# The first pair's down product as seven block products in a second last stage

## The chip, the cores and the metric

One core of a Trainium2 chip runs the whole kernel. The metric is the device time of one execution in microseconds. Five engines run side by side, each in the order of its own queue, and wait for one another by semaphores: TensorE (PE in the profile, with PEld for its weight loads), VectorE (DVE), ScalarE (ACT), GpSimd (POOL) and SyncE (SP), which here only issues transfers. A transfer between DRAM and SBUF is issued by SP, or by ScalarE's queue, and moved by 16 DMA engines.

## The reference

A transformer block on 2048 tokens of width 512 with six modulation vectors made from `c`: layer norm, linear attention with 32 heads, a gated residual, layer norm again, and a bilinear feed-forward part with 1376 hidden columns, again with a gated residual. The change touches the last part alone:

```python
h = _layernorm(x, axis=-1) * (1 + cb) + sb
g = jnp.einsum("bsd,df->bsf", h, w_gate)
u = jnp.einsum("bsd,df->bsf", h, w_up)
x = x + gb * jnp.einsum("bsf,fd->bsd", g * u, w_down)
```

All is float32.

## The kernel before

**Split operands.** A float32 operand is split into a high part (a copy into the fp32r type, on ScalarE) and a low part (the difference, on VectorE or GpSimd). A product is three matmuls: high by high, high by low, low by high (`split`, L201).

**Chunks, pairs, f tiles.** The tokens are four chunks of 512 (four tiles of 128). The hidden columns are eleven f tiles, 0 to 9 of 128 and 10 of 96. For the first pair of chunks (0, 1) the f tiles 8, 9 and 10 are done earlier, chunk by chunk (`gate_up`, `down`). The rest runs in the generator `ffn` (L1316): eight steps for the first pair with f tiles 0 to 7, then eleven steps for the second pair (2, 3) in the order `LATE`.

**A step** (`block`, L1183) makes gate and up of one f tile for both chunks of a pair. Two by two blocks (chunk by half of the width on the left, half of the width by gate or up on the right) are multiplied with seven block products where the plain way has eight. Each is six matmuls (`times`, L1160): a step has 42. Its left operands, "side parts", are a11, a12, a22 and the sums s1 to s4, each for two k tiles and in two parts. Its right operands, a "right", are b11, b21, b22 and the differences t1 to t4, held in seven tiles. A step uses four PSUM banks a, b, c, d: ScalarE copies a to b, b to c, and d and b to SBUF, VectorE adds and multiplies. With `raw` the result h stays whole, otherwise it is split by `flush` at the next step. The set of banks is `banks`, or `others` where `on` says so.

**Points and plan.** After each of the seven products the generator yields; the points "p1", "p5", "p6", "p2", "p7", "p3", "p4" are the places after product 1 to 7 at which `more` and `plan` put other work. `gates` (L1302) puts there: at p7 the load of the right of step m + 2 and the split of that of step m + 1, at p4 the differences of that of step m + 2 (GpSimd). In the first pair's steps p1 parks the right in DRAM (seven transfers); `Fetched` reads it back for the second pair.

**The first pair's down product.** After every two steps `down_group` (L1240) multiplies the two f tiles of h by w_down, plainly, 24 matmuls of 512 columns per chunk, and `evac` adds the result to x on VectorE; the groups of chunk 0 and chunk 1 are put behind later steps. The rows of w_down are loaded by `draw_load`, scaled by `gb` on VectorE, split on ScalarE and GpSimd.

**The second pair** keeps the h of all eleven f tiles. `planned` (L1497) puts the preparation of its w_down parts at points of its steps: five pairs of f tiles, each made into b11, b21, b22, t1 to t4 and parked. Its side parts a11, a12, s1, s2, s3 are also parked in DRAM (`aside`, `stash`) during the first pair's steps and read back before its own. `run` (L1576) is the last stage: its seven block products over five pairs of f tiles, six in a turned form with 512 columns (`turned`, L1481), the last with 256 columns (`product`, `mm`, L1461). For the turned ones the result is turned back by 32 by 32 blocks and moved by blocks to the output, after x was read back the same way (`x_blocks`, `flip`, `finish`). Its fetches from DRAM all go through SP's queue, in the order of the code.

Of the kernel before, what the change touches and what calls it, by code (L numbers as in the profile page):

```python
# [8 lines left out]
F32 = mybir.dt.float32  # L9
# [15 lines left out]
def tile_adaln_block(  # L25
# [1214 lines left out]
    def down_group(ch, side, js, outs, ds, last, by_tile=False, end=False):  # L1240

        hs = [out[side] for out in outs]

        def mm(ps, i, j, c, d):
            (hh, hl), (dh, dl) = hs[i], ds[i]
            a, b = j * P, (j + 1) * P
            n = hh.shape[0]
            nc.tensor.matmul(ps, hh[:, a:b], dh[:n, c:d], start=i == 0, stop=False)  # L1248
            nc.tensor.matmul(ps, hh[:, a:b], dl[:n, c:d], start=False, stop=False)  # L1249
            nc.tensor.matmul(ps, hl[:, a:b], dh[:n, c:d], start=False, stop=i == len(hs) - 1)  # L1250

        dn = {j: acc_bank() for j in js}
        tail = js[-1:] if end else []
        order = [(i, j) for i in range(len(hs)) for j in js if j not in tail]
        if by_tile:
            order.sort(key=lambda ij: ij[1])
        for i, j in order:
            mm(dn[j], i, j, 0, D)

        def take():  # L1260
            evac(ch, dn, [j for j in js if j not in tail], last)
            for j in tail:
                other = acc_bank()
                for ps, c, d in ((dn[j], 0, D // 2), (other, D // 2, D)):
                    for i in range(len(hs)):
                        mm(ps[:, c:d], i, j, c, d)
                    evac(ch, {j: ps}, [j], last, ((c, d),))
        return take

    groups = [((0, 1), g) for g in ((0, 1), (2, 3), (4, 5), (6, 7))]  # L1270
    steps = [(cs, f) for cs, g in groups for f in g]
    LATE = (10, 8, 9, *range(8))
    FIRST_AGAIN = len(steps) + 3
    steps += [((2, 3), f) for f in LATE]
    rights = {}

    def right_load(n):
        if n < FIRST_AGAIN:
            rights[n] = Right(steps[n][1])

    def right_sums(n, on=None):
        if n < FIRST_AGAIN:
            rights[n].sums(on)

    def right_split(n, on=None):
        if n < FIRST_AGAIN:
            rights[n].high()
            rights[n].lows(on)

    draws = {}  # L1290

    def draw_load(n):
        if n < len(steps):
# [626 lines left out]
```

## Time and profile before

| | us |
|---|---|
| median of three runs | 537.68 (537.64 to 537.89) |
| profiled execution | 538.41 |
| its span in the trace | 536.3 |
| TensorE busy | 530.6 |
| first pair's steps, with what runs among them | 251.7 to 363.3 |
| last stage, its first to its last matmul | 479.1 to 532.7 |

The profile's times count from the start of the span. The granted clock of TensorE was 1.00. A group of instructions is told by its line, engine, operation and operands, with its count, busy time and mean duration; a row of a timeline has start, length, engine, line and count; "SPq" is SP issuing a transfer, and "idle before" names what ended the wait.

### The profile page before, as it was taken

To read this page: it belongs to the slowest core of one execution; us is meant where nothing else is said; L and a number is where in the kernel's file an instruction comes from. 1 tells how busy PE (TensorE), PEld (TensorE's weight loads), DVE (VectorE), ACT (ScalarE), POOL (GpSimd) and SP (SyncE) were. 2 spreads that over 40 slices of the span, in tenths; PEclk is the share of its full clock that TensorE was granted. 3 is DMA by queue.
4 is the path that set the end of the run, shared out by engine and by line. 5 is a ranking of instruction groups with operands and counts; after the bars stand their busy time and mean duration, and the time that the engine had idled before them with its cause. 6 is when DMAs were issued, how large, how long until landed. Compare 5 with 4: busy or idle time off the path is not lost.

```text
span 536.3 us, 7850 instructions
## 1 busy us (share of the span) xinstructions
PE 530.6 (99%) x2407; PEld 436.9 (81%) x2407; DVE 406.3 (76%) x692; ACT 308.4 (58%) x584; POOL 157.0 (29%) x169
## 2 busy tenths in 40 slices
PE   8999999999999999999999999999999999999997
PEld 6888888888878878878888888887888888888886
DVE  7998878999999888779766577895646465569584
ACT  3696878769577774577584544554433434345530
POOL 2001010000012220076696677655632222310000
PEclk9999999999999999999999999999999999999999
DMA  8912426220075255857869687797189999589875
GB/s 271 385 50 76 160 94 212 89 78 2 30 210 177 61 199 154 281 167 217 275 187 337 227 297 238 261 350 232 61 281 326 400 383 367 198 265 285 268 166 140
DMA packets 102489, 113.39 MB, mean 211 GB/s; under 512 B 26480, under 2 KB 57712, under 8 KB 102448
## 3 DMA queue, kind: packets, MB, share of 16 engines
q1 hardware_dynamic: 98096, 111.85, 63.4%
q10 hardware_dynamic: 4352, 1.05, 0.9%
q8 instruction: 19, 0.31, 0.2%
q14 instruction: 22, 0.18, 0.1%
HBM read 68.03 MB, written 44.83 MB: 210 GB/s over the span
## 4 chain that ended last, share of the span: by engine, by line
PE 93%; DVE 4%; ACT 2%; issue 0%; ACTq 0%; DVEq 0%
PE bank L1165 27%; PE acc L882 8%; PE acc L1165 7%; PE bank L1489 4%; PE acc L1489 4%; PE bank L217 3%; PE bank L216 3%; PE bank L215 3%; PE acc L1249 3%; PE acc L1248 3%; PE acc L1250 3%; PE acc L424 3%; PE acc L423 3%; PE acc L422 3%; PE bank L965 2%; PE bank L967 2%
## 5 line engine op out<-in xcount | busy, mean ns | idle before, releaser
L1165 PE MATMUL bank<-h,w 128*128 128x512 f32 (+1 forms) x630 | 145.3, 389 | 0.0
L1165 PEld LDWEIGHTS bank<-h,w 128*128 128x128 f32 (+1 forms) x630 | 117.0, 186 | 25.9
L1170 ACT ACTIVATE bank<-bank 128x512 f32<-128x512 f32 (+1 forms) x32 | 18.7, 584 | 76.7 <-PE bank L1165 73.4
L203 DVE TENSOR_TENSOR kl<-u,kh 128x512 fp32r<-128x512 f32 (+1 forms) x38 | 26.4, 742 | 29.7 <-ACT kh L202 24.5
L271 POOL TENSOR_TENSOR rstd<-ve,half 128x2 f32<-128x2 f32 (+3 forms) x13 | 11.8, 910 | 108.1 <-DVE ve L270 64.9
L217 PE MATMUL bank<-w,h 128*128 128x512 f32 x104 | 40.7, 391 | 0.0
L215 PE MATMUL bank<-w,h 128*128 128x512 f32 x104 | 40.7, 391 | 0.0
L216 PE MATMUL bank<-w,h 128*128 128x512 f32 x104 | 40.5, 390 | 0.0
L1165 PE MATMUL acc<-h,w 128*128 128x512 f32 x168 | 38.7, 389 | 0.0
L203 POOL TENSOR_TENSOR w<-raw,w 128x512 fp32r<-128x512 f32 (+1 forms) x15 | 22.3, 1494 | 51.6 <-ACT w L202 46.5
L882 PE MATMUL acc<-w,xh 128*128 128x512 f32 x120 | 37.3, 392 | 0.0
L1165 PEld LDWEIGHTS acc<-h,w 128*128 128x128 f32 x168 | 31.5, 188 | 6.5
L1127 POOL TENSOR_TENSOR w<-raw,w 128x256 fp32r<-128x256 f32 (+3 forms) x22 | 24.3, 1104 | 37.2 <-ACT w L1120 37.2
L952 DVE TENSOR_TENSOR x<-acc,x 128x512 f32<-128x512 f32 x40 | 26.4, 685 | 11.1 <-PE acc L1250 11.1
L1127 POOL TENSOR_TENSOR w<-t,w 128x512 fp32r<-128x512 f32 (+1 forms) x22 | 29.2, 1329 | 0.0
L882 PEld LDWEIGHTS acc<-w,xh 128*128 128x128 f32 x120 | 22.4, 188 | 5.0 <-DVE w L793 0.3
L422 PE MATMUL acc<-kh,xh 128*128 128x512 f32 x64 | 25.1, 393 | 0.0
L424 PE MATMUL acc<-kl,xh 128*128 128x512 f32 x64 | 25.0, 390 | 0.0
L423 PE MATMUL acc<-kh,xl 128*128 128x512 f32 x64 | 25.0, 390 | 0.0
L1248 PE MATMUL acc<-w,kh 128*128 128x512 f32 x64 | 24.9, 389 | 0.0
L1250 PE MATMUL acc<-w,kl 128*128 128x512 f32 x64 | 24.9, 389 | 0.0
L1249 PE MATMUL acc<-w,kh 128*128 128x512 f32 x64 | 24.9, 389 | 0.0
(265 smaller groups left out, 1304.6 us busy)
## 6 DMA issues: line engine op xcount, KB each, us to landing
right<-w SPq DMA_DIRECT2D x56, 256.0 KB, 3.8
w<-right SPq DMA_DIRECT2D x56, 256.0 KB, 5.1
raw<-in_w_mod_dram SPq DMA_DIRECT2D x24, 256.0 KB, 4.0
raw<-in_B_w_down_dram SPq DMA_DIRECT2D x20, 256.0 KB, 4.0
down_t<-w SPq DMA_DIRECT2D x20, 256.0 KB, 5.1
w<-down_t SPq DMA_DIRECT2D x20, 256.0 KB, 5.3
x<-in_A_x_dram SPq DMA_DIRECT2D x16, 256.0 KB, 5.5
down_b<-w SPq DMA_DIRECT2D x15, 256.0 KB, 5.2
```

The lines of the kernel that those rows point to most:

```text
L203: (low or nc.vector).tensor_tensor(l, src, f32(h), op=ALU.subtract)
L215: nc.tensor.matmul(ps, ah, bh, start=i == 0, stop=False)
L216: nc.tensor.matmul(ps, ah, bl, start=False, stop=False)
L217: nc.tensor.matmul(ps, al, bh, start=False, stop=i == n - 1)
L422: nc.tensor.matmul(tacc[k], xh[:, a:b], kh, start=first, stop=False)
L423: nc.tensor.matmul(tacc[k], xl[:, a:b], kh, start=False, stop=False)
L424: nc.tensor.matmul(tacc[k], xh[:, a:b], kl, start=False, stop=last)
L882: nc.tensor.matmul(yps[i], x, y, start=False, stop=k == KD - 1 and x is al, skip_group_check=True)
L1127: sub = lambda out, x, y: (on or nc.gpsimd).tensor_tensor(out, x, f32(y), op=ALU.subtract)
L1165: mm = lambda x, y, **kw: nc.tensor.matmul(ps, x[:, k], y, skip_group_check=True, **kw)
L1248: nc.tensor.matmul(ps, hh[:, a:b], dh[:n, c:d], start=i == 0, stop=False)
L1489: nc.tensor.matmul(ps, of[:, x], y, start=start, stop=False, skip_group_check=True)
```

## The change

The eight f tiles of the first pair are no longer multiplied by w_down in groups between the steps. Each step's h (two tiles) is parked in DRAM. After the second pair's last stage a second one, `run_late`, multiplies them by the second pair's parked w_down parts: four pairs of f tiles ((0, 1), (2, 3), (4, 5), (7, 6)), seven block products. Four are "narrow": three matmuls of 256 columns for each pair and token tile. Three are "wide": one of 512 columns (the high part of h against both parts of w side by side) and one of 256, the two halves being added by VectorE. The results are added to x by half rows and stored.

With it come:

- the order `LATE` starts with f tile 7, whose right stays in SBUF (`KEPT`); the pair (7, 6) comes last
- the first pair's h is `raw`; its odd steps from the fourth on use `others`
- the second pair's side parts go into SBUF (`split_in`) and are not parked
- x of chunk 0 is parked in DRAM early and read back in the last stage
- the low parts of the rights of steps 4 and 6, of the odd f tile's w_down and of its first pair's parts are made on VectorE, not on GpSimd; the low parts of every other pair in the late stage on GpSimd
- all w_down parts are stored in the order that the turned form needs; the additions of the narrow products undo it by a stride of two
- in `run`, the late stage's first operands are fetched (a11 and b11 after the fourth product is issued; a12, a21, b21, a22 and x of chunk 0 after the sixth), a11 is split, and s1 and s3 are made by VectorE among its last additions

```diff
-    groups = [((0, 1), g) for g in ((0, 1), (2, 3), (4, 5), (6, 7))]
-    steps = [(cs, f) for cs, g in groups for f in g]
-    LATE = (10, 8, 9, *range(8))
-    FIRST_AGAIN = len(steps) + 3
-    steps += [((2, 3), f) for f in LATE]
+    FIRST = tuple(range(8))
+    LATE = (7, 10, 8, 9, *range(7))
+    ODD, LAST = 10, (7, 6)
+    steps = [((0, 1), f) for f in FIRST] + [((2, 3), f) for f in LATE]
+    FIRST_AGAIN = len(steps) - 7
+    KEPT = len(FIRST)
...
-            rights[n].lows(on)
+            rights[n].lows(nc.vector if n in ON_VECTOR else on)
+    ON_VECTOR = (4, 6)
...
-        if free[0] and parts:
-            takes = [down_group(*p) for p in parts.pop(0)]
-            yield
-            for take in takes:
-                take()
+    def h_park(f, out):
+        h_parked[f] = []
+        for n, x in enumerate(out):
+            h_parked[f].append(tc.dram_tile([P, D], F32, name=f"h_{f}_{n}"))
+            nc.sync.dma_start(h_parked[f][n], x)
...
+        pairs = list(zip(LATE[2:-1:2], LATE[3:-1:2])) + [LAST]
+        wide_down = Down((2, 3), pairs, KEPT)
+        late_down = Down((0, 1), pairs[1:], KEPT, wide_down)
...
+        for m, (cs, f) in enumerate(steps[:KEPT]):
+            out = []
+            more = {}
+            if m < KEPT - 1:
+                more["p1"] = [lambda: rights[m].park(f)]
+            if m:
+                more["p5"] = [lambda: h_park(*before)]
+            if m == 2:
+                others.extend(acc_bank() for _ in range(4))
+            yield from gates(m, cs, side, out, more, raw=True, on=others if m > 2 and m % 2 else None)
+            before = f, out
...
-        wide_down.run()
+        wide_down.run(late_down)
+        late_down.run_late(others[2:])
...
+        def h_fetch(self, n, side):
+            for fs in self.fs:
+                self.h.setdefault(fs[n], [None] * 2)[side] = load(h_parked[fs[n]][side], "u")
...
-                split(self.a(i, name), h, l)
+                split(self.a(i, name), h, l, nc.gpsimd if self.of and i % 2 else None)
...
             self.turned(d, "s1", "t1", True)
+            then.h_fetch(0, 0)
+            then.w_fetch("b11")
             self.h_split("s3", *pairs)
...
             self.turned(d, "s4", "b22", False, (0, 1))
+            then.h_fetch(1, 0)
+            then.h_fetch(0, 1)
+            then.w_fetch("b21")
+            then.h_fetch(1, 1)
+            xts[then.cs[0]] = [load(to, "x") for to in x_parked]
             self.finish(p5, c1, 1, nc.scalar)
             u2 = self.flip(onto(d, u2))
             self.finish(u2, c0, 1, nc.scalar)
+            then.h_split("a11", *range(then.NI))
...
                         if i % 2 == 0:
                             nc.sync.dma_start(ov(c1, i)[:, :HALF], x(i))
+                    for i in range(then.NI):
+                        then.h_sum("s1", i)
+                        then.h_sum("s3", i)
             add(*before)
+
+        def run_late(self, C):
...
+            self.h_split("a12", *pairs)
+            self.w_fetch("t2")
+            narrow("a11", "b11", True)
+            self.drop("a11", "b11")
+            self.h_next("s2", 0, 1)
+            add(c0, 0, C, js)
+            self.w_fetch("t1")
+            wide("a12", "b21", True)
+            self.drop("a12", "b21")
+            self.h_next("s2", 2, 3)
+            add(c0, 0, A, js, True)
+            self.w_fetch("t3")
+            narrow("s2", "t2", False)
+            self.drop("s2", "t2")
+            self.h_split("s1", *pairs)
+            add(c0, 1, C, js)
+            self.w_fetch("b22")
+            wide("s1", "t1", True)
+            self.drop("s1", "t1")
+            self.h_split("s3", *pairs)
+            self.h_next("s4", 0)
+            add(c1, 1, A, js)
+            self.w_fetch("t4")
+            narrow("s3", "t3", False)
+            self.drop("s3", "t3")
+            self.h_next("s4", 1, 2, 3)
+            add(c1, 1, C, js, True)
+            wide("s4", "b22", False)
+            self.drop("s4", "b22")
+            self.h_split("a22", *pairs)
+            add(c0, 1, A, js, True)
+            before = []
+            for j in (0, 2, 1, 3):
+                narrow("a22", "t4", False, (j,))
+                add(c1, 0, C, before, True)
+                before = (j,)
+            add(c1, 0, C, before, True)
```

More of the change, by code (lines that the diff above doesn't have):

```diff
@@ L1238, in block @@
         yield
[L1240 to L1268, printed above, removed]
@@ L1299, in tile_adaln_block @@
     free = [False]
-    parts = []
     def gates(m, cs, A, out, more, raw=False, on=None):
@@ L1342, in ffn @@
         for n, f in enumerate(LATE):
+            m = KEPT + n
             out = wide_down.h.setdefault(f, [])
[L1344 to L1348 removed]
+            more = {}
+            if n == 0:
+                more["p5"] = [lambda: h_park(*before)]
```

135 lines of the change are left out of this document (72 added, 63 removed).

## The prediction

> **What bounds the kernel now.** I read the page first, then the chain of work that ended last in order of time, then the instructions of one engine after another in the last 60 us, and the busy time by stretches.
>
> ```profile
> span 536.3 us, 7850 instructions
> PE 530.6 (99%) x2407; PEld 436.9 (81%) x2407; DVE 406.3 (76%) x692; ACT 308.4 (58%) x584; POOL 157.0 (29%) x169
> ...
> L1248 PE MATMUL acc<-w,kh 128*128 128x512 f32 x64 | 24.9, 389 | 0.0
> L1250 PE MATMUL acc<-w,kl 128*128 128x512 f32 x64 | 24.9, 389 | 0.0
> L1249 PE MATMUL acc<-w,kh 128*128 128x512 f32 x64 | 24.9, 389 | 0.0
> ```
>
> TensorE is busy for 99% of the span. The 389 ns of one matmul overlap with the next, so the price of a matmul is read from the chain, where runs of them stand with start, length and count:
>
> ```profile
> 259.87 23.12 PE bank L1165 x102
> ...
> 288.43 9.52 PE bank L1165 x42
> ...
> 303.38 9.53 PE bank L1165 x42
> ...
> 469.55 9.52 PE bank L1165 x42
> 479.06 3.40 PE acc L1489 x15
> ...
> 524.06 8.63 PE acc L1468 x72
> 532.72 0.42 DVE x L1639
> ```
>
> A step of the gate and up products (42 matmuls of 512 columns) takes 9.52 us, 0.2267 us each. From 288.43 to 303.38 there are 14.95 us: 42 matmuls of a step and 24 of the down groups (66 x 0.2267 = 14.96). So TensorE never waits between these steps; a wait that the change brings is paid in full. The 72 matmuls of 256 columns at L1468 take 8.63 us, 0.1199 us each, a little over half of 0.2267.
>
> **The change: TensorE.** Removed are the 64 + 64 + 64 = 192 matmuls of the first pair's down product: 192 x 0.2267 = 43.53 us. Added are seven products of four f pairs and four token tiles. Four are narrow: 4 x 4 x 4 x 3 = 192 matmuls of 256 columns. Three are wide: 3 x 16 = 48 of 512 columns (high part of h against both parts of w) and 48 of 256. That is 240 x 0.1199 + 48 x 0.2267 = 28.78 + 10.88 = 39.66 us. TensorE saves 3.87 us. Widths of 512 and 256 in turn don't stand in this trace. From below such a pair costs one and a half of 0.2267, 0.3400; from above two of it, 0.4534. I take the sum of the two rows, 0.3466, nearest to which both kinds stand by themselves; the ends are 0.3 us less and 5.1 us more over 48 pairs.
>
> By the Trainium skill, "TensorE: Matmul & The Clock Gate", section "Back-to-back issue gap", a matmul of N columns follows the one before after N/2.4 + 2.5 ns, that is 215.8 and 109.2 ns; the saving would then be an estimated 41.4 - 36.6 = 4.9 us. The trace disagrees with both gaps (226.7 and 119.9 ns), and the trace is used.
>
> The end stays: after the last matmul one 256-column add and its store, as now (532.72 to the span's end at 536.3).
>
> **First stage: less cover for the same side work.** Without the down groups the eight first steps last 9.52 us each where they had about 15. The stretch below holds the y products and steps 0 to 7 with their down groups.
>
> ```profile
> core 0: us, PE busy (x) PEld busy (x) DVE busy (x) ACT busy (x) POOL busy (x), PEclk, DMA share, GB/s
> 251.70:363.30 111.60, 111.60 (x494) 92.24 (x493) 83.54 (x124) 61.89 (x117) 73.55 (x69) 1.00 0.82 276
> ...
> 402.90:460.00 57.10, 57.10 (x254) 47.28 (x253) 31.64 (x53) 22.47 (x49) 15.90 (x22) 1.00 1.00 366
> ```
> ```profile
> L952 DVE TENSOR_TENSOR x<-acc,x 128x512 f32<-128x512 f32 x25 | 16.5, 686 | 5.7 <-PE acc L1250 5.7
> L203 DVE TENSOR_TENSOR kl<-u,kh 128x512 fp32r<-128x512 f32 x14 | 11.1, 834 | 9.5 <-ACT kh L202 9.5
> ...
> L203 DVE TENSOR_TENSOR h<-s,h 128x512 fp32r<-128x512 f32 x11 | 9.4, 880 | 0.1
> ...
> L1328 DVE TENSOR_TENSOR raw<-raw,row 128x512 f32<-128x512 f32 x8 | 5.3, 667 | 0.0
> ```
> ```profile
> L203 POOL TENSOR_TENSOR w<-raw,w 128x512 fp32r<-128x512 f32 x8 | 12.6, 1581 | 0.0
> ```
>
> It shrinks to about 2.7 + 8 x 9.52 = 79 us. VectorE loses the additions to x (L952, 16.5), the low parts of h (11.1) and the scaling of w_down (5.3), and takes over the low parts of two rights (8 operations, some 5 us): 83.5 - 32.9 + 5 = 56 of 79 us. ScalarE loses the copies that go before these low parts. GpSimd loses the 8 w_down splits (12.6) and two rights' low parts (some 9): 52. None becomes the bound on average. The transfers lose 28 side tiles (14 out, 14 back) and 8 of w_down, and gain 14 parked h tiles; at 0.262 MB a tile 276 GB/s x 111.6 us = 30.8 MB become about 25. By the row a full share moves 276/0.82 = 337 GB/s, so 25 MB take 74 of 79 us: nearly full, as the second stretch already is (share 1.00) without a wait of TensorE. The queue of SP is the thing to follow: it issues in order, and a right's loads stand behind the parking of another right.
>
> ```profile
> 286.01 4.25 SPq L1142 DMA_DIRECT2D right<-w  x7
> 290.35 0.84 SPq L116 DMA_DIRECT2D raw<-in_B_w_down_dram  x1
> 291.28 0.40 SPq L1103 DMA_DIRECT2D raw<-in_B_w_gate_dram  x1
> ```
> ```profile
> raw<-in_B_w_gate_dram SPq DMA_DIRECT2D x20, 128.0 KB, 3.8
> ...
> u<-stowed SPq DMA_DIRECT2D x8, 256.0 KB, 5.0
> ```
> ```profile
> 295.72 1.30 POOL L1127 TENSOR_TENSOR w<-t,w 128x512 fp32r<-128x512 f32 x1
> ...
> 300.73 0.74 POOL L1109 TENSOR_TENSOR t<-raw 128x256 f32<-128x256 f32 x1
> ```
>
> Take right 5. Two h tiles replace the w_down load ahead of it, so its four loads end at 293.7 and land 3.8 us later, at 297.5. GpSimd (right 4's low parts are now VectorE's) does four differences at about 0.72 by 300.4, then the low parts at 0.72 and 1.25 each: b11 at 301.1, t1 and t2 at 302.4. Step 5 begins at 251.71 + 2.72 + 5 x 9.52 = 302.0 and needs b11's low part two matmuls later, at 302.5: 1.3 us to spare. A landing after 5.0 us instead of 3.8 just eats that; I take 0.3 us for the whole stage, with 0 and 2.7 us as ends. The side parts of the second pair keep their place by step, so they are now made in less time: step 6 has four operations on banks at 0.69 and eight sums and low parts at 0.88 (the h<-s row), 2.8 + 7.0 = 9.8 us of VectorE in 9.52; step 7 has 2.8 + 7 x 0.88 = 9.0 and makes the 0.3 good. Alternate steps use other banks, so TensorE does not feel that lag: 0, and up to 1 us.
>
> **The handover, where I expect the price.** The late stage's second product reads the parts of a12, whose low parts VectorE makes after eight sums (s1, s3) that need the a21 and a22 halves of h, fetched from DRAM. These fetches are put on SP's queue behind the last moves of the stage before.
>
> ```profile
> GB/s 271 385 50 76 160 94 212 89 78 2 30 210 177 61 199 154 281 167 217 275 187 337 227 297 238 261 350 232 61 281 326 400 383 367 198 265 285 268 166 140
> ```
> ```profile
> 480.95 6.24 SPq L1413 DMA_DIRECT2D w<-down_t  x10
> ...
> 504.22 2.28 SPq L1413 DMA_DIRECT2D w<-down_t  x5
> 506.55 9.35 SPq L1550 DMA_DIRECT2D x<-x_rows  x16
> 517.00 3.85 SPq L1550 DMA_DIRECT2D c<-t  x8
> 520.96 4.26 SPq L116 DMA_DIRECT2D u<-c  x4
> ```
> ```profile
> w<-down_t SPq DMA_DIRECT2D x20, 256.0 KB, 5.3
> ...
> c<-t SPq DMA_DIRECT2D x8, 64.0 KB, 1.8
> ```
> ```profile
> 481.24 3.09 DVE L203 TENSOR_TENSOR kl<-u,kh 128x512 fp32r<-128x512 f32 x5
> ...
> 527.21 0.41 DVE L1639 TENSOR_TENSOR x<-x,acc 128x256 f32<-128x256 f32 x1
> 528.40 0.42 DVE L1639 TENSOR_TENSOR x<-x,acc 128x256 f32<-128x256 f32 x1 [0.78 <-PE acc L1468]
> 528.74 1.42 DVE L1650 TENSOR_TENSOR x<-x,u 128x256 f32<-128x256 f32 x4
> ```
>
> All in the old trace's clock. Eight new issues (a11 and b11 of the late stage) stand ahead of the 504.22 row; at its 2.28/5 = 0.456 us each that is 3.65 us. So x_rows ends at 515.90 + 3.65 = 519.5, c<-t (ready since 517.0) at 523.4, u<-c at 527.6. Then come 16 fetches of 256 KB: a12, a21, b21, a22. At 400 GB/s, which the slices of the page reach in the long stretch of fetches, one takes 0.655 us; with 1.8 us for the first, the landing time of c<-t, the sixteenth lands at 527.6 + 1.8 + 15 x 0.655 = 539.2. VectorE meanwhile reaches the sums at about 530.4 (the 528.74 row's end after two low parts at 3.09/5 = 0.62 more, of which the 0.78 idle takes a part) and would be through at 535.3. With the last tile at 539.2 the last two sums end at 540.5, two additions of 0.33 behind them at 541.1 and a12's first low part at 541.8. TensorE ends its first late product at 532.69 + 48 x 0.1199 = 538.45 and wants that part one wide matmul later, at 538.7. Wait: 541.8 - 538.7 = 3.1 us. What is queued behind the sums on VectorE are the last two additions of the second pair and all low parts that TensorE asks for; TensorE waits for these.
>
> The ends of this cost: if SP does not slip (u<-c at 525.2) and issues at 0.456, the sixteenth lands at 525.2 + 16 x 0.456 + 1.8 = 534.3, before VectorE is through, and the wait is 0 (below nothing it can't go, the product isn't shortened). If 16 issues go at 6.24/10 = 0.62 and the last lands 5.3 later, it is there at 527.6 + 9.3 + 5.3 = 542.2, and the wait is 6.0. I take 3.1, which goes by the rate of the transfers themselves.
>
> Behind it: VectorE has 8 sums of 0.62, 16 low parts of 0.62 (8 go to GpSimd) and 40 half additions of 0.33 in 39.7 us, 28 us; each next operand is then 1.4 to 2.5 us early. I take 0 there, up to 1.
>
> Sum, against the profiled execution of 538.41 (536.3 and 2.1 around it): 538.41 - 3.87 + 3.1 + 0.3 = 537.94. That execution lies 0.73 above the median 537.68, so on the median's scale **537.2**.
>
> **Rivals.** Fetches in time: the wait at the handover is 0 to 1.2 us and the first stage waits nowhere. For it: 402.90 to 460.00 shows full transfers and no wait; against it: 28 new issues on a queue that is already busy there. 537.68 - 3.87 + 0.3 = 534.1.
>
> Slower, by the supply of rights in the first stage: a step now carries 7 + 2 tiles and 0.52 MB of loads, 2.88 MB or 8.5 us at 337 GB/s; step 3 has the 1.05 MB that are fetched back for the flips (11.6 us) and step 5 the stores of x (10.1 us). If loads queue behind these stores for the excess over 9.52, 2.1 + 0.6 = 2.7 us come on top of the 3.1: 537.68 - 3.87 + 3.1 + 2.7 = 539.6. It decides once a right lands 1.3 us later than counted. Against it: parking may lag without harm, and no right is loaded for step 8.
>
> Slower, by a colder TensorE after the handover: the trace has such a start once.
>
> ```profile
> 2.00 8.44 PE acc L149 x24
> ```
>
> The first 24 matmuls of the kernel, of 512 columns, took 0.352 us each, 3.0 us more than 24 x 0.2267. If a wait of 4.2 us (the landing 1.1 later than taken) is followed by such a start: 537.68 - 3.87 + 4.2 + 3.0 + 0.3 = 541.3. Nothing in the trace shows whether a pause of that length does it. The same page of the Trainium skill, section "Part 1: The HAM clock gate", says that a pause of about 3.4 us or more halves the clock; by that rule the 3.1 taken stays just short of it.
>
> That the change doesn't save what it says: not likely, since both widths are in the trace.
>
> **How the numbers follow.** Forecast (handover wait between 1.8 and 4.5): 0.40, its own range 535.9 to 538.6. In time: 0.30. Supply of rights: 0.20. Cold start: 0.10. A measurement of this kernel tells from no change about 0.2%, 1.1 us: faster is under 536.6, slower over 538.8. Faster: 0.30 and a quarter of the forecast's 0.40 make 0.40; slower: 0.30 and a little of the forecast's late end, 0.32; within: 0.28. Range 533.9 to 541.0.
>
> **What would show it.** Right: steps 0 to 7 at 9.52 us without a gap; matmuls of the late products at 0.120 and 0.227; one gap of TensorE of about 3 us at the second late product, ended by a low part of VectorE that stood behind sums waiting for a fetched tile. Wrong: no gap there (then 534), gaps at the starts of steps 3 to 7 ended by GpSimd or a right's load (then 539 or more), or first matmuls after the gap at twice 0.2267.

## The result, and the profile after

The changed kernel takes 567.0 us (median of four runs, 565.54 to 567.69) beside 537.67 us of the kernel before on the same chip: ratio 1.0541, 95% interval 1.052 to 1.0562. The forecast was 537.2, its range 533.9 to 541.0. The profiled execution is the one of 567.69 us, with a span of 566.0.

From its page, the head, the busy time of TensorE and two rows of the forty slices:

```profile
span 566.0 us, 8107 instructions
...
PE 532.2 (94%) x2503; PEld 440.6 (78%) x2503; DVE 421.5 (74%) x727; ACT 312.5 (55%) x588; POOL 143.4 (25%) x154
...
PE   8999999999999999999998999989999999905997
...
PEclk9999999999999999999998999999999999966999
```

TensorE is busy for 532.2 us but for 94% of the span: it waits some 34 us, most of it in one place, slices 36 and 37, where the granted clock falls as well. The chain of waits has the place (start, length, what):

```profile
445.31 3.40 PE acc L1463 x15
...
490.31 4.31 PE acc L1442 x36
...
504.34 5.31 DMA u<-h
509.67 3.12 DMA out_dram<-t
512.80 1.66 ACT kh L202 x3
...
515.74 0.42 DVE x L1628
516.21 11.19 PE acc L1442 x80
...
545.55 5.75 PE acc L1442 x48
551.30 0.23 PE bank L1671
...
556.95 5.77 PE acc L1442 x48
```

The span is split at the first matmul of the last two stages. Before, that is 479.06, or 435.53 once the removed 43.53 us of down groups are taken out; from there 57.24 us are left, or 96.90 with the 39.66 us of the added products. After, it is 445.31 with 120.7 us left. So the first part lost 9.8 us and the last two stages 23.8: -3.87 + 9.8 + 23.8 = 29.7, the difference of the spans. The 3.87 goes into this split as it was forecast; that it is there is seen from the products themselves. A narrow one takes 5.75 us (the row at 545.55), and a wide one 5.65 us (from 551.30 to 556.95, sixteen pairs of a 512 and a 256 at 0.353): 4 x 5.75 + 3 x 5.65 = 39.95 us where 39.66 were forecast. In all runs below these two numbers are given: the start of the last two stages (435.5 would be no loss) and what follows it (96.9).

**The handover.** Four engines around the gap, from the timelines of the changed kernel:

```profile
494.33 0.28 PE L1442 MATMUL acc<-w,kl 96*128 96x256 f32 x1
516.21 0.79 PE L1442 MATMUL acc<-w,kh 128*128 128x256 f32 x2 [21.60 <-DVE x L1628]
...
513.44 0.69 DVE L203 TENSOR_TENSOR kl<-u,kh 128x512 fp32r<-128x512 f32 x1 [19.90 <-ACT kh L202]
...
515.74 0.74 DVE L1628 TENSOR_TENSOR x<-x,acc 128x256 f32<-128x256 f32 x2
...
487.61 25.12 ACTq L1530 DMA_DIRECT2D out_dram<-t  x16
512.78 3.75 ACT L202 ACTIVATE kh<-u 128x512 fp32r<-128x512 f32 x7 [29.98 <-DMA out_dram<-t]
...
494.98 4.02 SPq L116 DMA_DIRECT2D u<-h  x8
...
504.94 2.40 SPq L116 DMA_DIRECT2D x<-x  x4
```

Read backwards: TensorE waits for an addition of the second pair (L1628), which frees a bank. It stands on VectorE behind two low parts of the late block's a11; they wait for ScalarE's high parts; and ScalarE, which had nothing to compute, stands for 25.12 us in sixteen output transfers (L1530). p5's eight run from 487.6 to 493.5; u2's eight are issued only from 507.7 on, after the last of SP's fetches (507.34). The row of these transfers stood in the trace of before too (11.81 us), with nothing behind it on ScalarE.

**The first stage.** Two of its steps, by the busy time in stretches (length, then busy us of each engine, granted clock, DMA share, GB/s), and what stands around the wait in the first of them:

```profile
293.68:307.32 13.64, 11.05 (x44) 8.73 (x42) 8.85 (x13) 8.25 (x15) 7.70 (x8) 0.89 0.98 333
...
366.23:378.51 12.28, 9.82 (x43) 7.80 (x42) 8.45 (x16) 4.52 (x10) 5.10 (x7) 1.00 0.89 295
```
```profile
304.59 2.93 PE L1165 MATMUL bank<-h,w 128*128 128x512 f32 x6 [2.59 <-DVE u L1227]
...
301.63 0.71 DVE L344 STREAM_TRANSPOSE wide<-u 128x512 f32<-128x512 f32 x1 [4.72 <-DMA u<-stowed]
...
288.40 4.45 SPq L1142 DMA_DIRECT2D right<-w  x7
...
296.83 1.88 SPq L116 DMA_DIRECT2D u<-stowed  x4
```

Steps 4 and 11 take 13.64 and 12.28 us for 9.52 us of matmuls. In step 4 VectorE stands 4.72 us at a transpose whose tile SP fetched only at 296.83, behind seven parked right tiles, two parked h tiles and four loads; the addition that TensorE needs is queued behind it. The six matmuls after the wait took 2.93 us instead of 1.36. In step 11 the pause is 2.46 us. The rest of the 9.8 us are 1.3 us ahead of step 0, which e1 to e3 don't have, and some 1.4 us in steps 6 and 7.

### The profile page after: what moved, and what is told of

It is laid out like the page before. It is cut to its first block, busy times and chain, and to the rows that moved or that the text cites. A ratio compares the mean times of both kernels' runs of the same rounds, so it can differ in the third digit from the quotient of the medians.

```text
span 566.0 us, 8107 instructions
## 1 busy us (share of the span) xinstructions
PE 532.2 (94%) x2503; PEld 440.6 (78%) x2503; DVE 421.5 (74%) x727; ACT 312.5 (55%) x588; POOL 143.4 (25%) x154
## 5 line engine op out<-in xcount | busy, mean ns | idle before, releaser
L1165 PE MATMUL bank<-h,w 128*128 128x512 f32 x462 | 108.3, 393 | 3.0 <-DVE u L1227 3.0
L1165 PEld LDWEIGHTS bank<-h,w 128*128 128x128 f32 x462 | 87.4, 190 | 22.0 <-DVE u L1227 3.9
L1165 PE MATMUL acc<-h,w 128*128 128x512 f32 (+1 forms) x336 | 78.4, 391 | 2.9 <-ACT acc L1170 2.9
L1165 PEld LDWEIGHTS acc<-h,w 128*128 128x128 f32 (+1 forms) x336 | 62.1, 185 | 18.1 <-ACT acc L1170 3.7
L1442 PE MATMUL acc<-w,kh 128*128 128x256 f32 x176 | 33.2, 291 | 21.6 <-DVE x L1628 21.6
L1442 PEld LDWEIGHTS acc<-w,kh 128*128 128x128 f32 x176 | 28.5, 198 | 22.0 <-DVE x L1628 21.8
L202 ACT ACTIVATE kh<-u 128x512 fp32r<-128x512 f32 (+1 forms) x38 | 21.1, 623 | 31.4 <-DMA out_dram<-t 30.0
L203 POOL TENSOR_TENSOR kl<-u,kh 128x512 fp32r<-128x512 f32 x8 | 11.8, 1506 | 82.3 <-ACT kh L202 82.3
L1170 ACT ACTIVATE bank<-bank 128x512 f32<-128x512 f32 x24 | 14.0, 582 | 33.4 <-PE bank L1165 30.1
L1442 PE MATMUL acc<-w,kl 128*128 128x256 f32 x88 | 25.4, 289 | 0.0
```

What stands on the lines that cost most here:

```text
L202: nc.scalar.activation(h, src, AF.Copy)
L203: (low or nc.vector).tensor_tensor(l, src, f32(h), op=ALU.subtract)
L1165: mm = lambda x, y, **kw: nc.tensor.matmul(ps, x[:, k], y, skip_group_check=True, **kw)
L1170: nc.scalar.activation(out, x, AF.Copy)
L1442: nc.tensor.matmul(ps, x[:, a:b], y, start=start, stop=False, skip_group_check=True)
```

## The experiments

Single executions but for the last three; the kernel before took 537.43 us beside e1 to e4, 538.21 beside e5 to e7 and 537.85 beside e8 and e9.

**Round one: four single edits.**

`e1`, u2's eight output transfers on SP:

```diff
-            self.finish(u2, c0, 1, nc.scalar)
+            self.finish(u2, c0, 1, nc.sync)
```

> The eight output transfers of the second pair's u2 are issued by SP instead of ScalarE; nothing else. Theory (a queue: a11's high copies stand on ScalarE behind transfers that wait for SP's twenty fetches): the 21.6 us pause of TensorE between the second and the third token tile of the second pair's last product shrinks to under 2 us, a11's high copies run near 494 instead of 513 us, and the cold matmuls behind the pause go with it (about 1.3 us). What comes next is the wait that the forecast had there: a12's low part behind the sums that wait for the fetched a21, some 4 us plus about 1.4 of half rate at the second late product. Span 566.0 - 23 + 5.5 = about 549. Rival (the late block reads its fetches too late, as the forecast had it, and the order on ScalarE doesn't matter): the pause stays near 21 us and the span near 566.

Measured: 554.57 us; stages begin at 443.4, 109.3 us follow. Rows of its TensorE, ScalarE and VectorE:

```profile
495.43 0.80 PE L1442 MATMUL acc<-w,kh 128*128 128x256 f32 x2 [2.74 <-DVE x L1628]
512.67 0.58 PE L1672 MATMUL bank<-w,kl 128*128 128x256 f32 x1 [4.11 <-DVE kl L203]
...
492.00 2.19 ACT L202 ACTIVATE kh<-u 128x512 fp32r<-128x512 f32 x4 [11.11 <-DMA out_dram<-t]
...
505.95 0.69 DVE L1404 TENSOR_TENSOR s<-u,u 128x512 f32<-128x512 f32 x1 [8.49 <-DMA u<-h]
...
511.93 1.29 DVE L203 TENSOR_TENSOR kl<-u,kh 128x512 fp32r<-128x512 f32 x2
```

The pause of 21.6 us is 2.74, and the wait of the forecast appears in its place: 4.11 us at the second late product, for low parts behind eight sums that waited 8.49 us for a fetched tile. The queue theory holds, the rival falls. The span is 552.7 us, 3.7 over the 549 expected although its first stage was 1.9 us shorter: behind both pauses TensorE ran at half rate for longer than taken (last section).

`e2`, the twenty fetches moved:

```diff
-            then.h_fetch(1, 0)
-            then.h_fetch(0, 1)
-            then.w_fetch("b21")
-            then.h_fetch(1, 1)
-            xts[then.cs[0]] = [load(to, "x") for to in x_parked]
             self.finish(p5, c1, 1, nc.scalar)
             u2 = self.flip(onto(d, u2))
             self.finish(u2, c0, 1, nc.scalar)
+            then.h_fetch(1, 0)
...
+            xts[then.cs[0]] = [load(to, "x") for to in x_parked]
```

> The twenty fetches of the late block stand in the program behind the additions and transfers of p5 and u2 instead of ahead of them; ScalarE still issues u2's transfers. In the built program the last of u2's eight transfers then waits for a completion count that the eleventh of the twenty fetches gives, where in the changed kernel it waits for the last ones. Theory (SP's and ScalarE's transfers take turns on eight completion counters in program order, and each waits for the one before it on its counter): the last of u2's transfers is issued when about eleven fetches have landed, near 494.5 + 11 x 0.62 + 1 = 502 instead of 512.7 us, a11's high copies end near 503, the pause of 21.6 us becomes about 11, span about 555. Rival (the transfers are late because the sixteen engines are full with the fetches, whoever comes first): as many bytes are to be moved, the last of u2's transfers is still issued after 507 us, span 563 or more.

Measured: 561.03 us; 443.0, then 116.3. The transfers ended at 505.5 (502 by the theory, after 507 by the rival), the pause was 16.7 us and the span 559.3 (555 and 563): between the two expectations. By its times alone it settles nothing; the semaphores of its trace, told under `e3`, do.

`e3`, a11's split moved:

```diff
+            then.h_split("a11", *range(then.NI))
             self.finish(p5, c1, 1, nc.scalar)
             u2 = self.flip(onto(d, u2))
             self.finish(u2, c0, 1, nc.scalar)
-            then.h_split("a11", *range(then.NI))
```

> The split of a11 for the late block stands ahead of p5's and u2's additions and transfers; nothing else. Theory (queue): the pause between the token tiles falls from 21.6 to under 2 us, as a11's copies no longer stand behind the transfers; but a12's copies still do on ScalarE, until about 513 us, and its low parts after that, so the wait moves to the second late product: 10 to 13 us there, span about 554 to 557. Rival (a11's own fetch, h(0,0), is what is late): the pause stays, span 566.

Measured: 560.63 us; 443.6, then 115.3.

```profile
493.96 0.51 PE L1442 MATMUL acc<-w,kh 128*128 128x256 f32 x2 [1.09 <-DVE x L1628]
...
516.90 0.80 PE L1671 MATMUL bank<-w,kh 128*128 128x512 f32 x1 [12.60 <-ACT kh L202]
...
506.01 10.16 ACTq L1530 DMA_DIRECT2D out_dram<-t  x16
```

As the theory had it: the pause falls to 1.09 us and comes back as 12.6 us at the second product, since a12's copies are still behind the transfers. Now all sixteen start at 506.0, p5's too, though their data was there at about 490: in the order of the built program they now stand behind the fetches. The trace records each transfer's semaphore, and the wait ahead of it. SP's and ScalarE's transfers share eight semaphores (100 to 107), and a transfer waits for the one that had its number before it. In the changed kernel u2's first transfer (507.70) waits on 107, which a fetch of h issued by SP at 502.26 has; in `e3` p5's first (506.01) also on 107, a fetch issued at 499.76; in `e2` u2's last (505.19) on 102, the eleventh of the twenty fetches, as expected there. So in this program a transfer on ScalarE's queue waits for earlier fetches of SP's, and with it all of ScalarE's work behind it.

`e4`, three moves in the first stage:

```diff
-            put(3, "p5", self.odd_turn)
+            put(2, "p2", self.odd_turn)
...
-    x_parked = []
-    for j in range(NJ):
-        x_parked.append(lift_out(f"x_{j}", xts[0][j]))
...
     stow(2, 0, 1, 2, 3)
+    x_parked = []
+    for j in range(NJ):
+        x_parked.append(lift_out(f"x_{j}", xts[0][j]))
...
-        (4, "p1"): [turned(1, 2, "a12")], (4, "p5"): [flips(3, 0)], (4, "p6"): [split_in(0, "a11"), flips(3, 1)],
+        (4, "p1"): [turned(1, 2, "a12")], (4, "p6"): [split_in(0, "a11")], (4, "p7"): [flips(3, 0), flips(3, 1)],
```

> First stage alone: the four transfers that park x stand behind the parking of h's last products instead of ahead of the load of the gate's rows; the two transposes of step 3's block stand at the end of step 4 instead of in its middle; the turning of the odd tile stands one step earlier. Theory (each wait of the first stage is a queue that the change made longer): step 0 begins 1.2 us earlier, step 4 falls from 13.64 to about 9.5 us, step 11 loses its wait of 2.46 us and the slow matmuls behind it (2.8 in all); the last stage begins near 445.3 - 8.1 = 437.2, the pause of 21.6 us at the handover stays, span about 558. Rival (the added transfers fill the DMA engines, so that the stage is late wherever they stand): steps 4 and 11 keep their lengths within 1 us, span 565 or more.

Measured: 562.53 us; 440.8, then 119.9. Step 4 fell to 10.06 us, but steps 6 and 7 rose to 11.74 and 10.77 and step 11 stayed at 11.73. A miss: 2.5 us won against e1 to e3 (443.0 to 443.6), not 8; the lateness moved on to the next steps. e1 to e3 also show that without any edit there the first stage starts the last two at 443.3, 2 us before the profiled execution of the changed kernel.

**Round two: what makes the first stage late.** `e5` leaves the parking of x and h out, `e6` VectorE's low parts of the second pair's left side; `e7` is another order of side work. All three have a11's split ahead, u2's transfers on SP, and (`e5`, `e7`) the sums behind a12's low parts:

```diff
-            h_parked[f].append(tc.dram_tile([P, D], F32, name=f"h_{f}_{n}"))
-            nc.sync.dma_start(h_parked[f][n], x)
+            h_parked[f].append(again[f][n] if f in again else again[6][2 + n])
...
-        x_parked.append(lift_out(f"x_{j}", xts[0][j]))
...
-            xts[then.cs[0]] = [load(to, "x") for to in x_parked]
+            xts[then.cs[0]] = [load(h_parked[f][0], "x") for f in range(4)]
```

That is e5's own part; e6's own part, and the part in which e5 and e7 share the late block:

```diff
+        def high(self, n):
+            h = B("h", dt=F32R)
+            nc.scalar.activation(h, self.f[n], AF.Copy)
+            self.done(n, h, h)
...
-    split_in = lambda k, n: lambda: second[k].into(second_side).split(n)
+    split_in = lambda k, n: lambda: second[k].into(second_side).high(n)
```
```diff
-                    for i in range(then.NI):
-                        then.h_sum("s1", i)
-                        then.h_sum("s3", i)
...
             self.h_split("a12", *pairs)
+            for i in pairs:
+                self.h_sum("s1", i)
+                self.h_sum("s3", i)
```

> Two separate parts. Handover mended: a11's split ahead of p5's and u2's additions, u2's transfers on SP, the eight sums s1 and s3 behind a12's low parts instead of ahead of them. If the two queues seen so far (ScalarE behind u2's transfers, VectorE's low parts behind the sums) are all there is, the pause between the token tiles is 1.1 us as in the kernel with a11's split moved, there is no wait at the second late product, and the stretch from the first matmul of the second last stage to the end of the span falls from 120.7 us to about 98. First stage: the parking of x and of h is left out (the late block fetches parts of rights instead, so its values are others). Theory A (the down matmuls that left were the cover for VectorE's and ScalarE's side work; parking matters little): of the 8.2 us that steps 4 to 11 lose, 5 or more remain, the last two stages begin at 440 or later, span 538 or more. Theory B (the parking fills SP's queue and the DMA engines): under 3 us remain, the stages begin by 438.5, span 536.5 or less.

> Two separate parts. First stage: VectorE's fourteen low parts of the second pair's left side are left out (the high parts are used in their place, so the values are others); parking stays. Theory A (VectorE's side work no longer fits into 9.52 us steps): what steps 4, 6 and 7 lose falls from about 5.5 to under 2 us together, step 11 keeps its 2 to 3 us, the last two stages begin near 439. Theory B (parking): they begin near 443 as in the runs of before. Handover: a11's split ahead and u2's transfers on SP, but the eight sums stay ahead of a12's low parts. The low part is then ready near 511 to 512 of that trace's clock as in the run with the transfers on SP, TensorE is there 4 us earlier: a wait of 6 to 8 us at the second late product and some 2.6 us of half rate behind it; 96.9 + 1.1 + 7 + 2.6 = 107.6 us from the first matmul of the second last stage to the end; span near 547.

> The mended handover (a11's split ahead, u2's transfers on SP, the sums behind a12's low parts) and another order of the first stage's side work: x parked later, the transposes of step 3's block later, the odd tile's turn one step earlier, w_down's raw tiles loaded one step point ahead of the parking that held SP up (so that their scaling at the head of step 11 waits for nothing), three splits moved from step 7 into step 8. Expected if the waits are queues: step 11 loses its 2 to 2.8 us wait, steps 6 and 7 lose under 1.5 us together, the last two stages begin near 437, and with 98 us from there the span is 535, the time 537, about that of the kernel before. If the first stage's loss is not a matter of order, they begin at 440 or later and the span is 538 or more.

Measured: e5 555.41 us, 438.4 and 115.3; e6 555.39, 442.9 and 110.8; e7 560.02, 440.8 and 117.3. Steps 4, 6, 7 and 11 of e5:

```profile
291.75:301.27 9.52, 9.52 (x44) 7.88 (x42) 6.00 (x10) 6.41 (x12) 6.12 (x7) 1.00 0.99 335
310.79:320.34 9.55, 9.55 (x43) 7.83 (x42) 9.10 (x13) 6.75 (x13) 6.53 (x7) 1.00 0.97 327
320.34:331.01 10.67, 9.87 (x44) 7.80 (x42) 10.11 (x13) 4.77 (x9) 6.58 (x6) 1.00 0.68 196
359.79:371.61 11.82, 9.82 (x44) 7.81 (x42) 8.44 (x16) 4.52 (x10) 5.08 (x7) 1.00 0.91 324
```

Without the parking steps 4 and 6 lose nothing; without the fourteen low parts nothing is won. So it is the parking (theory B), not VectorE's load; which of the two, x's or h's, is not separated. Step 11 is a matter of its own. e7's other order of side work left the first stage at 440.8, by its expectation the sign that order does not matter; e9 below finds an order that does.

At the handover e5 and e7 missed by 17 and 19 us, and e6 by 3 (a pause of 8.2 us where 6 to 8 were expected, but ended by ScalarE). e7:

```profile
502.90 6.20 ACTq L1530 DMA_DIRECT2D out_dram<-t  x8
...
509.83 0.79 PE L1668 MATMUL bank<-w,kh 128*128 128x512 f32 x1 [8.30 <-ACT kh L202]
```

Only p5's eight transfers were left on ScalarE, with data ready at 487.1; standing behind the fetches in program order, they began at 502.90. It is the same wait again: in the changed kernel these eight ran at 487.6 to 493.5, ahead of the same fetches.

**Round three: no transfer on ScalarE, and SP in another order.** `e8` issues the sixteen transfers from SP behind t1 and t3; in the first stage it is e7 with x stored for the flip in steps 8 to 10 and GpSimd making the first w_down pair's low parts. `e9` adds to that:

```diff
-        at = {"p7": [lambda: right_load(m + 2), lambda: right_split(m + 1)], "p4": [lambda: right_sums(m + 2)]}
+        at = {"p1": [lambda: right_load(m + 2)], "p7": [lambda: right_split(m + 1)], "p4": [lambda: right_sums(m + 2)]}
...
-            at[point] = [*does, *at.get(point, ())]
+            at[point] = [*at.get(point, ()), *does] if point == "p1" else [*does, *at.get(point, ())]
...
-                more["p5"] = [lambda: h_park(*before)]
+                more["p2"] = [lambda: h_park(*before)]
```

> The handover with no transfer on ScalarE at all: a11's split ahead, the sixteen output transfers of p5 and u2 issued by SP behind the late block's t1 and t3 fetches, the eight sums behind a12's low parts. Theory (two queues: ScalarE's copies behind transfers that wait for SP's fetches, VectorE's low parts behind sums that wait for a fetch): pause of 1.1 us between the token tiles, none over 1 us behind it, 97 to 99.5 us from the first matmul of the second last stage to the end of the span (120.7 in the changed kernel, 117.5 in the run that left p5's transfers on ScalarE). Rival (something else holds the late block, the fetch of t2 or of a12 itself): one more pause of 3 us or more, 103 or more. First stage: as in the run with the other order of side work, and the eight stores of x for the flip go from steps 5 to 8 into steps 8 to 10, where the DMA share is 0.15, and GpSimd makes the low parts of the first w_down pair again, as in the kernel before. If SP's queue and the full DMA engines make the loss of steps 5 to 7, half of it goes; step 11 falls to 10 us or less if VectorE's 3.3 us subtraction beside GpSimd was its cause. Stages begin near 438, span near 536.

> As the run before, and in every step of the first stage SP issues the next right's four loads ahead of the parking of seven right tiles, and the parking of h two products later. Same bytes, another order on SP. If it is the order that makes the loss (loads wait behind parking, 4.4 us in a step), steps 4 to 7 lose under 1 us together and the last two stages begin near 436.5. If it is the bytes (DMA engines full from 284 to 327 us), nothing is won against the run before: 437.5 to 438.5. If tiles run short (the loads hold two more of them for 6 us), it gets worse: 440 or more.

Measured: e8 547.38 us, 440.2 and 105.4; e9 544.39 us, 437.1 and 105.6. Rows of e8:

```profile
490.57 0.50 PE L1443 MATMUL acc<-w,kh 128*128 128x256 f32 x2 [1.09 <-DVE x L1632]
511.10 0.77 PE L1443 MATMUL acc<-w,kh 128*128 128x256 f32 x2 [4.55 <-DVE x L1659]
...
501.73 0.69 DVE L1405 TENSOR_TENSOR s<-u,u 128x512 f32<-128x512 f32 x1 [4.93 <-DMA u<-h]
...
510.25 1.41 DVE L1659 TENSOR_TENSOR x<-x,acc 128x256 f32<-128x256 f32 x4
```

With ScalarE free, 11.9 us come back against e7, and one pause stays, at the third late product: the additions that free its banks stand on VectorE behind the sums, which wait for the fetch of a22. So e8 came out at the rival's number, by VectorE's queue and not by t2 or a12. That pause is nearly all that its late block loses: 4.55 us, and the product behind it takes 8.4 us instead of 5.75, for most of it at half rate. e8's first stage missed too (440.2, near 438 expected). There the order on SP alone (e8 to e9, the same bytes) is worth 3.1 us: steps 4, 6 and 7 of e9 take 9.52, 9.52 and 9.83. What is left is step 11, 11.03 us:

```profile
360.06 7.48 DVE L1351 TENSOR_TENSOR raw<-raw,row 128x512 f32<-128x512 f32 x2
...
360.31 1.30 POOL L1127 TENSOR_TENSOR w<-raw,w 128x512 fp32r<-128x512 f32 x1
361.56 1.29 POOL L1127 TENSOR_TENSOR w<-t,w 128x512 fp32r<-128x512 f32 x1
```

**Round four: VectorE.** `e10` gives the four s3 sums to GpSimd, puts the additions ahead of the s2 parts, runs the third product pair by pair, and scales the second w_down pair a step earlier. `e11` keeps s3 on VectorE but behind the third product and makes right 11's low parts on VectorE. `e12` fetches h and b21 ahead of the round trip of c21 (a block that is stored to DRAM and read back). One line or group of each:

```diff
-                self.h_sum("s3", i)
+                self.h_sum("s3", i, on=nc.gpsimd)
```
```diff
-    ON_VECTOR = (4, 6)
+    ON_VECTOR = (4, 6, 11)
```
```diff
+            then.h_fetch(1, 0)
+            then.h_fetch(0, 1)
+            then.w_fetch("b21")
+            then.h_fetch(1, 1)
             c21 = tc.dram_tile([CH, D], F32, name="c21")
```

> Against the run before: in the late block the fetch of a22 ahead of b21's, the four s3 sums on GpSimd, the additions of the first late product ahead of the s2 parts, the third product pair by pair instead of token tile by token tile (the same matmuls in another order); in the first stage the load and the scaling of the second w_down pair one step earlier. Theory (the 4.7 us pause at the third late product is VectorE's queue: eight sums that wait for a fetch, then eight more operations, then the additions that free the banks): the pause falls to 1.5 us or less, no half rate behind it, 97.5 to 99.5 us from the first matmul of the second last stage to the end. If instead the fetch of t2 or x is what the product waits for, the pause stays over 3 us. First stage: the two scalings that took 7.5 us beside GpSimd leave step 11, which falls from 11.0 to 10 us or less; the last two stages begin near 436. Span near 534.5, time near 536.3, that is 0.2 to 0.3% under the kernel before.

> The two stages as in the run that loads ahead of the parking, with these changes. First stage: the low parts of right 11 on VectorE instead of GpSimd. If VectorE's 7.5 us for two scalings in step 11 come from GpSimd running beside it without a pause, they fall to about 2 us and step 11 from 11.03 to under 10.3 us; if they come from something else, step 11 gets longer by the 2.5 us that VectorE takes over. Late block: before the third product only the four s1 sums, the s2 parts into new tiles, the s3 sums behind the third product, the additions that free the banks ahead of the s2 parts, the low parts of s1 ahead of the next additions, the third product pair by pair. Theory (the pause there is VectorE's queue, and GpSimd's sums in the run before doubled VectorE's durations): no pause over 1.5 us after the one of 1.1, 98 to 101 us from the first matmul of the second last stage to the end, span 535 to 538, time 537 to 540, no slower than 0.4% over the kernel before. If VectorE's total in the late block is simply too much (about 41 us for 39.7 of matmuls), pauses come back further on, 103 us or more.

> First stage as in the run before. Handover: the twelve h tiles and b21 of the late block are fetched ahead of the round trip of c21 instead of behind it, x and t2 right behind that; the additions of c21 and their stores go to the end of the late block; s1 and s3 both ahead of the third product on VectorE again, the order otherwise as in the run before. Theory (the late block starts VectorE's sums 6 to 7 us late, at 498.4 where VectorE was free from 492.3, because the fetch of a22 lands then; all pauses of the late block follow from that, as VectorE has about as much to do there as TensorE): the sums run from about 492 to 498, no pause over 1 us stands behind the one of 1.1 us, 98 to 101 us from the first matmul of the second last stage to the end (108.4 in the run before), span 534 to 537, time 536 to 538.5: about the kernel before. If the tiles run short (the fetches wait for tiles that c21's path holds), the fetches land as late as before and it stays at 104 or more.

Measured against the kernel before: e10 544.3 us, ratio 1.0113 (1.0096 to 1.013), 438.1 and 105.3; e11 545.91 us, 1.0152 (1.0135 to 1.0169), 435.7 and 108.4; e12 542.99 us, 1.0094 (1.0077 to 1.011), 435.9 and 105.5.

The first stage is mended in e11: 435.7, step 11 at 9.52 us, the two scalings at 1.90 us now that right 11's low parts are off GpSimd. (In e10 the two still took 8.33 us beside GpSimd, and step 11 11.66.) From e11, its scalings, its four s1 sums, and the same four of e10 with GpSimd's four beside them:

```profile
362.33 1.90 DVE L1351 TENSOR_TENSOR raw<-raw,row 128x512 f32<-128x512 f32 x2
...
498.41 2.73 DVE L1405 TENSOR_TENSOR s<-u,u 128x512 f32<-128x512 f32 x4 [6.08 <-DMA u<-h]
```
```profile
496.07 4.82 DVE L1405 TENSOR_TENSOR s<-u,u 128x512 f32<-128x512 f32 x4 [0.23 <-DMA u<-h]
...
496.84 6.44 POOL L1405 TENSOR_TENSOR u<-u,u 128x512 f32<-128x512 f32 x4 [1.55 <-DVE s L1405]
```

The late block is not: e10 missed its 97.5 to 99.5 us, the other two their 98 to 101. In e10 the third product has no pause any more, but the fourth has one of 1.91 us. In e11 the third product waits for the fetch of t2, not for VectorE, and runs at half rate behind it. In e12 VectorE's sums start at 494.8 instead of 498.4 (about 492 was expected) and the pauses behind them are 1.01 us or less, but the token tiles' pause is 1.98. A row of e11's TensorE, then one of e12's with the stretches of its late block:

```profile
505.05 0.72 PE L1443 MATMUL acc<-w,kh 128*128 128x256 f32 x2 [2.44 <-DMA w<-down_t]
```
```profile
519.64 0.47 PE L1443 MATMUL acc<-w,kh 128*128 128x256 f32 x2 [1.01 <-DMA w<-down_t]
...
487.20:493.20 6.00, 6.00 (x38) 6.00 (x39) 0.66 (x2) 0.00 (x0) 0.00 (x0) 0.72 1.07 353
...
493.50:537.80 44.30, 41.53 (x286) 37.49 (x284) 38.56 (x77) 11.23 (x20) 8.57 (x6) 1.00 0.75 230
```

VectorE is busy for 38.56 of 44.3 us, in a block whose matmuls need 39.66. Of e12's 8.6 us over 96.9, some 3.5 lie ahead of the late block, whose first product starts at 493.05 (the pause of 1.98 and the slow matmuls behind it, 0.72 of the clock), and some 4.5 in it, spread over many short waits. The longest, 1.01 us, is for the fetch of t3. SP issues it at 513.99, behind four stores of x that wait for VectorE's additions until 511.19 and after. So VectorE's queue reaches TensorE there through SP's; how much of the 4.5 us comes that way stays open. No version beats the kernel before.

## Why the prediction was wrong

- **TensorE saves 3.87 us**: right to 0.3 us. 48 narrow matmuls take 5.75 us (0.1198 each); a pair of 512 and 256 takes 0.353 where 0.3466 was taken, so 43.53 - 39.95 = 3.6 us are saved.
- **First stage 0.3 us, ends 0 and 2.7**: 9.8 measured in this profile, near 8 in e1 to e3. The step named SP's queue and followed one right through it. Its 337 GB/s for a full share was low (its own second row has 366 at a share of 1.00), but not what failed. It took for granted that the other users of that queue could lag; the fetch for the flips stood behind the same parking, and VectorE's in-order queue carried its delay to TensorE. The rival "supply of rights" came nearest (loads queued behind stores), and priced it at 2.7 by the excess bytes of two steps. That the parking is it, e5 shows; that its order matters and not only its bytes, e9 (3.1 us).
- **Step 11** was not in the prediction. In the changed kernel it waits for a w_down load late on SP; once that is early, VectorE's scaling is slow beside GpSimd (7.48 us, against 1.90 in e11).
- **Handover 3.1 us at the second late product, ends 0 and 6.0**: 23.8 measured for the two stages, 21.6 of it one pause at another place, between the token tiles, and some 1.5 the half rate behind it. This is the step that failed. It listed what is queued behind the sums on VectorE and the fetches on SP, and left out ScalarE's queue: a11's split was moved behind sixteen transfers there, and twenty fetches were put ahead of the last eight of them. The wait that it did name exists, with its place and chain: 4.11 us in e1, when the other is gone.
- **Late chain 0, up to 1**: right for the changed kernel, with less room than counted. Its late block runs from 521.95 to 562.72, 40.8 us where 39.66 were forecast, and its one listed wait is 0.44 us. The 28 us of VectorE were sized too small: 24 sums and low parts at 0.68, 16 additions at 1.41/4 and 24 at 3.23/8 make 32. The versions that move the eight sums s1 and s3 into the late block (e5, e7 to e9, e11 and e12) make it 37, and e12 shows 38.56, nearly TensorE's 39.66: what starts VectorE late is then hardly made good.
- **Cold TensorE**: the rival's mechanism is there, and the margin ("the 3.1 taken stays just short of it") is no safe one: see the last section.
- **Saved as said**: even with the first stage free of loss and the transfers off ScalarE, e12 stays 0.9% behind. TensorE's work did shrink; what the last two stages still lose, 8.6 us, is more than that.

## What to carry to other kernels

For each instruction that a change adds or moves, write down what stands ahead of it on its own engine, the transfers that a computing engine issues included, and what each of those waits for: here a copy of 0.6 us stood 20 us behind transfers that TensorE's path had nothing to do with. Matmuls that are taken away were also the cover for side work and transfers; price the shorter step by everything that waits on the shared queue, not by one item followed through it. An engine's total in a new block is counted by operation before it is called free, and a saving of 4 us is weighed against the first pause of 2 us.

## What the runs showed of the hardware

- **Half rate after short pauses.** In the changed kernel a pause of 2.59 us was enough, in e12 one of 1.98 us. Length alone does not decide: in step 11 of the changed kernel the clock stayed at 1.00 behind a pause of 2.46 us (the row from 366.23 on, above), and in the same step a pause of 2.04 us brought half rate in e1 while one of 2.05 us did not in e2. In e1, stretches from behind the pauses of 2.74 and 4.11 us:

```profile
495.40:501.30 5.90, 5.88 (x27) 5.88 (x28) 2.06 (x5) 2.52 (x4) 2.73 (x3) 0.50 0.96 326
501.30:508.10 6.80, 6.80 (x59) 6.80 (x58) 2.08 (x4) 0.00 (x0) 0.59 (x1) 1.00 1.05 394
...
512.70:518.60 5.90, 5.90 (x19) 5.09 (x20) 5.80 (x12) 2.08 (x4) 0.00 (x0) 0.52 0.85 280
```

  The granted clock is 0.50 and 0.52 for 5.9 us, so each of these two pauses costs nearly 3 us more than its length; behind the pause of 21.6 us it was only 3.2 us. The Trainium skill, "TensorE: Matmul & The Clock Gate", section "Part 1: The HAM clock gate", puts the fall to half rate at an idle window of about 3.4 us. Pauses well below that were enough here, and the measurement decides. It also says that the windows run free; that fits pauses of one length going either way, and the different lengths of the half rate.

- **VectorE beside GpSimd.** In e9 two 128x512 operations with both inputs in SBUF, the scalings, took 7.48 us. The first alone took 6.87, and beside it seven GpSimd operations ran one right behind the other. In e11 GpSimd had no pause beside the scalings either, and they took 1.90 us, while two of its operations took 1.20 us instead of 0.75. What decides which side waits, these runs do not show. Four sums on each side by side took 4.82 and 6.44 us (e10), eight in a row on VectorE 5.4 (e12, eight at 0.68): nothing was won by sharing them out. The Trainium skill, "GPSIMD Engine Reference", section "1. Specifications", says that GpSimd shares its SBUF interfaces with VectorE, in contention with VectorE's instructions that read two inputs from SBUF; these rows agree that the two hold each other up.
